# First batch's column sums in two tiles, early small work on two engines, and other steps for three pieces of side work in a fused attention and FFN kernel

## The chip, the cores and the metric

The kernel runs on one core of one Trainium2 chip. The metric is the device time of one execution in microseconds (us); "before" is the median of three runs.

## What is computed

Four batches of q, k and v, each 6080 x 256, go through an attention over channels, and its result through a two-layer FFN with squared ReLU:

```python
qn = q / (np.linalg.norm(q, axis=1, keepdims=True) + 1e-06)
kn = k / (np.linalg.norm(k, axis=1, keepdims=True) + 1e-06)
s = kn.transpose(0, 2, 1) @ qn / tau
s = s - s.max(-1, keepdims=True)
a = np.exp(s)
a /= a.sum(-1, keepdims=True) + 1e-09
x = (v @ a).reshape(B * S, D)
h = np.maximum(x @ w_in, 0.0)
out = h * h @ w_out            # w_in 256 x 2048, w_out 2048 x 256, both float64
```

The norms run over the 6080 rows, so each needs the sum of squares of a whole column of q or k.

## The kernel before

Since `x @ w_in = v @ (a @ w_in)`, each batch first forms the 256 x 256 product of k and q (the "gram"), the softmax from it, and W = a @ w_in; then the 6080 rows of v pass in 12 blocks of up to 512 rows through W, ReLU, square and w_out. Every product is taken from high and low parts (fp32r), except the gram of the first batch and of the first five chunks of the second (the "heads"), which are plain float32.

**Start (`start_first`).** q and k of batch 0 come in 25 chunks of 512 KB (the last two smaller), one k and one q transfer each, all issued by SP; SP's issues wait for the landing of the transfer eight places before. Ten chunk buffers are used in turn, so chunk c + 9 is asked for at step c. Per chunk TensorE makes four 128x256 products into `gram` (each shown as two matmuls in the trace), ScalarE squares the chunk (`squares`, chunk 0 straight into the tile `acc`, the others into a tile "x" with two buffers), and VectorE adds the square to `acc` (`add_squares`, one step later). In between, w_in's first 1 MB piece is loaded and decoded from float64 (`Weights.load`, `Weights.stage`, `decode`), a few instructions at a time. The products of the last three chunks are kept back (`rest`).

**Softmax and W (`softmax_and_W(0)`, lines 403 to 540).** VectorE adds the two halves of `acc`; TensorE sums it over the partitions (`ps_n`); a chain of small VectorE operations makes the norms, then come scaling, exponential, transposes (`ps_t`) and W's first quarter (`ps_w`). While TensorE would wait it is given the kept-back products and the ten rows of the heads (`head_products`; a row is two products, so four matmuls of the trace); the list `beside_first` says at which step of the chain, and the loop at lines 771 and 772 issues the two rows that are left before the blocks begin.

**Blocks.** The order is one list of steps, each a block's 128 columns of the hidden layer (`first_product`: six 128x512 matmuls into `ps_h`). Two steps are a pair. ScalarE takes ReLU from PSUM (x), squares a pair, and copies its high part (`g_hi`); VectorE subtracts for the low part (`g_lo`); two pairs later TensorE multiplies by w_out into `ps_o`. The first two blocks (32 steps, `PAIR`) use w_out directly, eight products per pair. From the third block on seven products per pair are used (`by_seven`): VectorE makes four sums of x's quarters, and TensorE needs seven combinations of w_out, four of which (`wS_hi`, `wS_lo`) are made once by `sums_of_w_out`: four groups of three steps (an addition; four short operations; ScalarE's copy to `wS_hi` with VectorE's subtraction to `wS_lo`). During the first two blocks the remaining pieces of w_in and w_out are decoded (`stages`), W's quarters are formed at steps 6, 14 and 22, the heads are squared and added (`head_squares`, one chunk per call) and `sums_of_w_out` follows: lines 812 and 813 call one or the other once per step after step 24. What is left goes on from step 32 (`beside`), one call per step except at two steps of each block, and then the attention of batch 1 (`attention(1)`) from its sixth chunk.

Each engine works its instructions in program order, so an instruction that waits holds all behind it on that engine.

Of the kernel before, what the change touches and what calls it, by code (L numbers as in the profile page):

```python
# [8 lines left out]
F32 = mybir.dt.float32  # L9
# [4 lines left out]
AF = mybir.ActivationFunctionType  # L14
# [16 lines left out]
def kernel(  # L31
# [22 lines left out]
    tensor, vector, scalar, pool_engine = (  # L54
        InProgramOrder(tc, e) for e in (nc.tensor, nc.vector, nc.scalar, nc.gpsimd)
    )
    P = 128
    B, N, C = q.shape
# [3 lines left out]
    T = 512  # L62
# [3 lines left out]
    J = 2  # L66
# [28 lines left out]
    const = ctx.enter_context(tc.tile_pool(name="const", bufs=1))  # L95
    wpool = ctx.enter_context(tc.tile_pool(name="wpool", bufs=NG))
    pool = ctx.enter_context(tc.tile_pool(name="pool", bufs=2))
    ps_acc = ctx.enter_context(tc.tile_pool(name="ps_acc", bufs=2, space=bass.MemoryType.PSUM))
    ps_h = ctx.enter_context(tc.tile_pool(name="ps_h", bufs=3, space=bass.MemoryType.PSUM))
# [4 lines left out]
    ones = const.tile([P, P], F32, name="ones")  # L104
# [3 lines left out]

    exp_bias = const.tile([P, 1], F32, name="exp_bias")
    vector.memset(exp_bias, -896.0 * 2.0**23)  # L110
    wo_hi = const.tile([P, NF, C], F32R, name="wo_hi")
    wo_lo = const.tile([P, NF, C], F32R, name="wo_lo")
    late = {}
# [126 lines left out]
    class Gram:  # L240
# [45 lines left out]
        def squares(self, c):  # L286
            p, jn, _ = self.q[c]
            if c == 0:
                self.acc = pool.tile([P, 2, J, C], F32, tag="acc", name=f"acc{self.b}", bufs=1)
                sq = self.acc  # L290
            else:

                sq = self.raws[c]
                if self.b == 0:
                    sq = pool.tile([P, 2, J, C], F32, tag="x", name=f"sq{self.b}_{c}")
                self.sq[c] = sq
            scalar.activation(sq[:p, :, :jn, :], self.raws[c][:p, :, :jn, :], AF.Square)

        def add_squares(self, c):
            p, jn, _ = self.q[c]  # L300
            if c in self.sq:
                a = self.acc[:p, :, :jn, :]
                vector.tensor_add(a, a, self.sq.pop(c)[:p, :, :jn, :])

    grams = {}
# [1 line left out]
    def start_first(b=0):  # L307

        g = grams[0] = Gram(0)
        total = g.n + HEAD  # L310
        AHEAD = len(FAST_TAGS) - 1

        room = pool.tile([P, HEAD - 1, 2, J, C], F32, tag="wS_lo", name="qk_heads", bufs=1)

        def load(c):
            if c == g.n:
                grams[1] = Gram(1)
            if c < g.n:
                g.load(c, FAST_TAGS[c % len(FAST_TAGS)])
            elif c < total and B > 1:  # L320
                grams[1].load(c - g.n, raw=room[:, c - g.n] if c - g.n < HEAD - 1 else None)

        for c in range(AHEAD):
            load(c)
        for c in range(g.n):
            if c < g.n - LAST:
                for _ in g.products(c, [(g.raws[c], g.raws[c])]):
                    pass
            g.squares(c)
            if c:  # L330
                g.add_squares(c - 1)
            load(c + AHEAD)
            if c in (2, 15):
                weights.load(int(c > 2))
            if c in (13, 14, 15, 17):
                weights.stage(0)
            if c == 19:
                load_v(*order[0])
        for c in range(g.n + AHEAD, total):
            load(c)  # L340
        g.add_squares(g.n - 1)

        def rest():
            for c in range(g.n - LAST, g.n):
                for _ in g.products(c, [(g.raws[c], g.raws[c])]):
                    pass
            yield

        return rest()

    def head_products():

        g = grams[1]
        for c in range(HEAD):
            yield from g.products(c, [(g.raws[c], g.raws[c])])

    def head_squares():
        g = grams[1]
        while g.raws:
            c = min(g.raws)  # L360
            g.squares(c)
            del g.raws[c]
            g.add_squares(c)
            yield
# [182 lines left out]
    def load_v(b, n, tag="v"):  # L547
        t0, tn = blocks[n]
        raw = pool.tile([P, NC, T], F32, tag=tag, name=f"v{b}_{n}", bufs=1)
        nc.sync.dma_start(raw[:, :, :tn], vT[b, :, t0 : t0 + tn].rearrange("(c p) t -> p c t", p=P))  # L550
        V[b, n] = [raw, None, None]
# [10 lines left out]
    def split_v_lo(b, n):  # L562
        tn = blocks[n][1]
        raw, hi, _ = V[b, n]
        V[b, n][2] = pool.tile([P, NC, T], F32R, tag="v_lo", name=f"v_lo{b}_{n}")
        vector.tensor_sub(V[b, n][2][:, :, :tn], raw[:, :, :tn], hi[:, :, :tn].bitcast(F32))
# [8 lines left out]
    def first_product(b, n, f):  # L575
        tn = blocks[n][1]
        _, v_hi, v_lo = V[b, n]
        w_hi, w_lo = W[b, f // FPG]
        f0 = (f % FPG) * P
        ps = ps_h.tile([P, T], F32, tag="h", name=f"ps_h{b}_{n}_{f}")  # L580
        parts = [(c, x, y) for x, y in ((w_hi, v_hi), (w_hi, v_lo), (w_lo, v_hi)) for c in range(NC)]
        for i, (c, wt, vt) in enumerate(parts):
            tensor.matmul(
                ps[:, :tn], wt[:, c, f0 : f0 + P], vt[:, c, :tn], start=i == 0, stop=i == len(parts) - 1
            )
        if f % 2 == 0:
            X[b, n, f // 2] = pool.tile([P, 8, tn // 2], F32, tag="x", name=f"x{b}_{n}_{f // 2}")
        x = X[b, n, f // 2].rearrange("p s t -> p (s t)")
        s = slice((f % 2) * tn, (f % 2 + 1) * tn)
        scalar.activation(x[:, s], ps[:, :tn], AF.Relu)  # L590
# [21 lines left out]
    def parts_of_sums(b, n, r):  # L612

        x = X.pop((b, n, r))
        hi, lo = G[b, n, r]
        if by_seven(b, n):
            hi, lo, src = hi[:, 3:7, :], lo[:, 3:7, :], x[:, 4:8, :]
        else:
            src = x[:, 0:4, :]
        scalar.copy(hi, src)  # L620
        vector.tensor_sub(lo, src, hi.bitcast(F32))
# [3 lines left out]
    def second_product(b, n, r, part):  # L625
        if by_seven(b, n):
            seven_products(b, n, r, part)
        else:
            eight_products(b, n, r, part)
# [115 lines left out]

    weights = Weights()
    rest = start_first()
    first = softmax_and_W(0)
    heads, squares_of_heads = (head_products(), head_squares()) if B > 1 else (iter(()), iter(()))
# [16 lines left out]
    while (0, 0) not in W:  # L766
# [1 line left out]
        for piece in beside_first.get(at, ()):  # L768
            piece()
        at += 1  # L770
    for _ in heads:
        pass


    stages = {0: [1, 2], 1: [2, 1], 2: [2, 2], 3: [2], 4: [2, 2], 5: [2]}
# [19 lines left out]
    for i in range(len(steps) + 2 * LAG):  # L795
        part = now["part"] = i % 2
        if i < len(steps):
            b, n, f = steps[i]
            at = b * NB + n
            first_product(b, n, f)  # L800
            if n == NB - 1 and f % FPG == FPG - 1:
                may_write_W.add((b + 1, f // FPG))

        if i >= PAIR:
            gens = (beside,)
        else:
            for item in stages.get(i, ()):
                weights.stage(item)
            if i == 1:
                split_v_lo(*order[1])  # L810
            gens = (first,) if i in steps_of_W else ()
            if i > 24:
                gens += (squares_of_heads if B > 1 and grams[1].raws else sums,)

        if i >= PAIR and steps[min(i, len(steps) - 1)][2] in (2 * LAG - 2, 2 * LAG - 1):
            gens = ()
        if i < PAIR or part == 0:
            for gen in gens:
                next(gen, None)
        if part == 0 and 0 <= i // 2 - 1 < len(pairs):  # L820
            parts_of_sums(*pairs[i // 2 - 1])
        if i in steps_of_W:
            next(first)
        if part == 1 and i // 2 < len(pairs):
            squares_and_sums(*pairs[i // 2])
        if part and late_work:
            if next(late_work[0], "end") == "end":
                late_work.pop(0)
        if i >= 2 * LAG:
            second_product(*pairs[i // 2 - LAG], part)  # L830
        if i < len(steps):
            at_hi, at_lo = (None, None) if at == 0 else (12, 13) if at == 1 else (6, 8)
            if i == 2 and len(order) > 2:
                load_v(*order[2])
            if f == at_hi and at + 1 < len(order):
                split_v_hi(*order[at + 1])
            if f == at_lo and at + 1 < len(order):
                split_v_lo(*order[at + 1])
                if at + 2 < len(order):
                    load_v(*order[at + 2])  # L840
        if i >= PAIR and part:
            for gen in gens:
                next(gen, None)
# [27 lines left out]
```

## Time and profile before

| | |
|---|---|
| median of 3 runs | 2225.31 us (2223.28 to 2227.23) |
| profiled execution, its own time | 2223.41 us |
| its span, first to last instruction | 2221.6 us |
| TensorE (PE) busy | 2207.7 us (99%) |
| ScalarE (ACT) busy | 1844.9 us (83%) |
| VectorE (DVE) busy | 1762.6 us (79%) |
| granted TensorE clock over the span | 1.000 |

The 1.8 us between span and time lie around the program. Nearly all instructions stand under line 27, the helper that issues them, so one goes by tile names and times. A matmul's shown duration overlaps the next one's; from one start to the next is what it costs.

### The profile page before, as it was taken

How to read it: one execution, taken by the hardware profiler on the slowest of the kernel's cores; microseconds unless marked ns; L12 is line 12 of the kernel's file. 1: busy time of each engine (PE TensorE's matmuls, PEld its weight loads, DVE VectorE, ACT ScalarE, POOL GpSimd, SP SyncE). 2: the span in 40 equal slices, each digit the busy share in tenths (PEclk: the TensorE clock that was granted, in tenths of full speed). 3: DMA queues.
4: the chain of work that ended last, by engine and by line, in shares of the span. 5: the costliest groups of instructions: out<-in, count | busy, mean ns of one | idle time of the engine just before them, and what ended most of it. 6: DMA issues, size and time to landing. Idle time of an engine off the chain costs nothing.

```text
span 2221.6 us, 34359 instructions
## 1 busy us (share of the span) xinstructions
PE 2207.7 (99%) x13740; PEld 1982.9 (89%) x13740; DVE 1762.6 (79%) x2470; ACT 1844.9 (83%) x2294; POOL 0.7 (0%) x6
## 2 busy tenths in 40 slices
PE   9999999999999999999999999999999999999999
PEld 7788999988989999988898999998899888888888
DVE  7868888888778888878777888887877787787783
ACT  5788888888788888888878888888887888888885
POOL 0000000000000000000000000000000000000000
PEclk9999999999999999999999999999999999999999
DMA  9510122110111112110121122110102010010000
GB/s 342 176 67 29 60 74 68 46 39 29 66 66 58 60 61 71 62 41 22 35 70 54 60 68 73 58 53 22 33 24 76 21 36 20 22 37 20 22 26 18
DMA packets 76495, 126.99 MB, mean 57 GB/s; under 512 B 7728, under 2 KB 34096, under 8 KB 76336
## 3 DMA queue, kind: packets, MB, share of 16 engines
q1 hardware_dynamic: 76336, 124.81, 17.2%
q8 instruction: 107, 1.75, 0.3%
q14 instruction: 52, 0.43, 0.1%
HBM read 95.68 MB, written 29.10 MB: 56 GB/s over the span
## 4 chain that ended last, share of the span: by engine, by line
PE 95%; DVE 3%; DMA 1%; ACT 1%; issue 0%; SPq 0%; DVEq 0%; ACTq 0%
PE ps_h L27 46%; PE ps_o L27 41%; PE gram L27 5%; PE ps_w L27 2%; DVE g_lo L27 1%; DMA qk<-in_k 1%; DVE acc L27 1%; DVE x L27 0%; ACT x L27 0%; DMA qk<-in_q 0%; ACT g_hi L27 0%; PE ps_n L27 0%; DVE o L27 0%; DVE dec_m L27 0%; DVE wo_sums L27 0%
## 5 line engine op out<-in xcount | busy, mean ns | idle before, releaser
L27 DVE TENSOR_TENSOR g_lo<-x,g_hi 128x768 fp32r<-128x768 f32 (+2 forms) x744 | 804.7, 1082 | 94.2 <-ACT g_hi L27 93.9
L27 DVE TENSOR_TENSOR x<-x 128x256 f32<-128x256 f32 (+3 forms) x1080 | 551.9, 511 | 276.9 <-ACT x L27 251.9
L27 ACT CAST g_hi<-x 128x768 fp32r<-128x768 f32 (+2 forms) x744 | 698.0, 938 | 23.4 <-DVE x L27 10.9
L27 ACT ACTIVATE x<-ps_h 128x512 f32<-128x512 f32 (+1 forms) x768 | 456.3, 594 | 298.9 <-PE ps_h L27 277.2
L27 PE MATMUL ps_h<-v_hi,w_hi 128*128 128x512 f32 (+1 forms) x1536 | 479.3, 393 | 0.0
L27 PE MATMUL ps_h<-v_hi,w_lo 128*128 128x512 f32 (+1 forms) x1536 | 477.5, 391 | 0.0
L27 PE MATMUL ps_h<-v_lo,w_hi 128*128 128x512 f32 (+1 forms) x1536 | 474.9, 390 | 0.0
L27 ACT ACTIVATE x<-x 128x1024 f32<-128x1024 f32 (+1 forms) x384 | 404.6, 1054 | 12.2
L27 PE MATMUL ps_o<-g_lo,wS_hi 128*128 128x256 f32 (+1 forms) x1440 | 402.7, 280 | 3.1 <-DVE g_lo L27 2.8
L27 PE MATMUL ps_o<-g_hi,wS_lo 128*128 128x256 f32 (+1 forms) x1440 | 401.6, 279 | 0.0
L27 PE MATMUL ps_o<-g_hi,wS_hi 128*128 128x256 f32 (+1 forms) x1440 | 401.1, 279 | 0.0
L27 PEld LDWEIGHTS ps_h<-v_lo,w_hi 128*128 128x128 f32 x1536 | 287.9, 187 | 65.4
L27 PEld LDWEIGHTS ps_h<-v_hi,w_lo 128*128 128x128 f32 x1536 | 288.5, 188 | 62.1
L27 PE MATMUL ps_o<-g_hi,wo_hi 128*128 128x256 f32 (+3 forms) x1176 | 330.6, 288 | 0.9 <-ACT g_hi L27 0.9
L27 PE MATMUL ps_o<-g_hi,wo_lo 128*128 128x256 f32 (+3 forms) x1176 | 330.7, 288 | 0.0
L27 PE MATMUL ps_o<-g_lo,wo_hi 128*128 128x256 f32 (+3 forms) x1176 | 330.4, 287 | 0.1
L27 PEld LDWEIGHTS ps_o<-g_lo,wS_hi 128*128 128x128 f32 x1440 | 271.1, 188 | 19.7 <-DVE g_lo L27 3.9
L27 PEld LDWEIGHTS ps_o<-g_hi,wS_hi 128*128 128x128 f32 x1440 | 270.4, 188 | 15.5
L27 PEld LDWEIGHTS ps_o<-g_hi,wS_lo 128*128 128x128 f32 x1440 | 270.6, 188 | 0.0
L27 PEld LDWEIGHTS ps_h<-v_hi,w_hi 128*128 128x128 f32 x1536 | 239.3, 188 | 4.9
L27 PEld LDWEIGHTS ps_o<-g_hi,wo_hi 128*128 128x128 f32 x1176 | 221.4, 188 | 17.4 <-ACT g_hi L27 1.4
L27 PEld LDWEIGHTS ps_o<-g_lo,wo_hi 128*128 128x128 f32 x1176 | 220.8, 188 | 16.7 <-DVE g_lo L27 0.5
(87 smaller groups left out, 1669.0 us busy)
## 6 DMA issues: line engine op xcount, KB each, us to landing
v<-in_vT SPq DMA_DIRECT2D x44, 512.0 KB, 3.8
qk<-in_k SPq DMA_DIRECT2D x87, 256.0 KB, 2.7
qk<-in_q SPq DMA_DIRECT2D x87, 256.0 KB, 3.0
out_T<-o SPq DMA_DIRECT2D x168, 128.0 KB, 1.7
wi_hi<-wi_kept SPq DMA_DIRECT2D x12, 512.0 KB, 3.3
wi_lo<-wi_kept SPq DMA_DIRECT2D x12, 512.0 KB, 4.1
w_raw<-in_w_in SPq DMA_DIRECT2D x4, 1024.0 KB, 5.2
w_raw<-in_w_out SPq DMA_DIRECT2D x4, 1024.0 KB, 5.4
```

The source lines that it names most:

```text
L27: return lambda *args, **kwargs: self.tc.keep_in_program_order(issue(*args, **kwargs))
```

## The change

```diff
@@ setup
     exp_bias = const.tile([P, 1], F32, name="exp_bias")
     vector.memset(exp_bias, -896.0 * 2.0**23)
+
+    for _ in range(7):
+        tensor.matmul(ps_h.tile([P, T], F32, tag="h", name="ps_first")[:, 0:P], ones, ones, start=True, stop=True)
+    scalar.activation(const.tile([P, 1], F32, name="first"), exp_bias, AF.Square)
@@ Gram.squares
             if c == 0:
                 self.acc = pool.tile([P, 2, J, C], F32, tag="acc", name=f"acc{self.b}", bufs=1)
+                self.accs = [self.acc]
                 sq = self.acc
+            elif c == 1 and self.b == 0:
+                sq = pool.tile([P, 2, J, C], F32, tag="g_hi", name=f"acc{self.b}_1")
+                self.accs.append(sq)
@@ Gram.add_squares
-                a = self.acc[:p, :, :jn, :]
+                a = self.accs[c % len(self.accs)][:p, :, :jn, :]
@@ start_first
-            if c in (2, 15):
-                weights.load(int(c > 2))
-            if c in (13, 14, 15, 17):
+            if c in (0, 15):
+                weights.load(int(c > 0))
+            if c in (12, 13, 14, 16):
                 weights.stage(0)
@@
         g.add_squares(g.n - 1)
+        vector.tensor_add(*g.accs[:1], *g.accs)
@@ main program
-    for _ in heads:
-        pass
@@ loop over steps
+            if i in (2, 3):
+                next(heads, None)
             gens = (first,) if i in steps_of_W else ()
-            if i > 24:
+            if i >= 16 and (i >= 24 or i % 2 == 0):
                 gens += (squares_of_heads if B > 1 and grams[1].raws else sums,)
```

In words: seven products of a tile of ones (fourteen matmuls in the trace) and one small square are issued ahead of the first q and k. In batch 0, squares of even chunks are added into one tile and those of odd chunks into another, and the two tiles are added at the end. w_in's first piece is asked for after chunk 9 rather than after chunk 11, and four of its decoding steps come one chunk earlier. The last two rows of the heads move into steps 2 and 3. The squares of the heads begin at step 16 (one in each even step, then one in each step from 24), so that the sums of w_out begin at step 25 rather than 30 and the attention of batch 1 five calls earlier.

Three places show how the instructions move. VectorE, the end of batch 0's sums, before (`acc` is the tile of sums, `sq_n` a chunk's squares):

```order
L27 TENSOR_TENSOR acc_132<-acc_132,sq_21_348 128x1024
L27 TENSOR_TENSOR acc_132<-acc_132,sq_22_351 128x1024
L27 TENSOR_TENSOR acc_132<-acc_132,sq_23_354 128x2x256
L27 TENSOR_TENSOR acc_132<-acc_132,sq_24_357 64x2x256
L27 TENSOR_TENSOR acc_132<-acc_132 128x2x256
```

and of the change (`acc_1_158` is the second tile):

```order
L27 TENSOR_TENSOR acc_148<-acc_148,sq_22_366 128x1024
L27 TENSOR_TENSOR acc_1_158<-acc_1_158,sq_23_369 128x2x256
L27 TENSOR_TENSOR acc_148<-acc_148,sq_24_372 64x2x256
L27 TENSOR_TENSOR acc_148<-acc_148,acc_1_158 128x1024
L27 TENSOR_TENSOR acc_148<-acc_148 128x2x256
```

Neighbouring additions go into different tiles now, and one full-size addition stands before the halves are added.

TensorE, from the heads to the fifth step of the blocks (`gram_301` and `gram_316` are batch 1's gram, `qk_4` the heads' last chunk), before:

```order
L27 MATMUL gram_301<-qk_heads 128x256 x4
L27 MATMUL gram_301<-qk_4_341 128x256 x4
L27 MATMUL ps_h_0_0_490<-v_hi_0_414,w_hi_0_458 128x512 x2
...
L27 MATMUL ps_h_0_2_519<-v_hi_0_414,w_lo_0_459 128x512 x2
L27 MATMUL ps_h_0_3_534<-v_hi_0_414,w_hi_0_458 128x512 x2
...
L27 MATMUL ps_h_1_0_547<-v_hi_1_447,w_hi_0_458 128x512 x2
```

and of the change:

```order
L27 MATMUL gram_316<-qk_heads 128x256 x4
L27 MATMUL ps_h_0_0_502<-v_hi_0_430,w_hi_0_474 128x512 x2
...
L27 MATMUL ps_h_0_2_531<-v_hi_0_430,w_lo_0_475 128x512 x2
L27 MATMUL gram_316<-qk_4_356 128x256 x2
L27 MATMUL ps_h_0_3_548<-v_hi_0_430,w_hi_0_474 128x512 x2
...
L27 MATMUL gram_316<-qk_4_356 128x256 x2
L27 MATMUL ps_h_1_0_563<-v_hi_1_463,w_hi_0_474 128x512 x2
```

The four products of `qk_4` stood ahead of the first `ps_h`; two now follow the third step and two the fourth.

VectorE, the last group of w_out's sums with no other work between the four short operations and the subtraction, before (fourth pair of the third block, `x_2_3`):

```order
L27 TENSOR_TENSOR x_2_3_1337<-x_2_3_1337 128x512
L27 TENSOR_TENSOR x_2_3_1337<-x_2_3_1337 128x256 x2
L27 TENSOR_TENSOR g_lo_2_3_1364<-x_2_3_1337,g_hi_2_3_1363 128x768
L27 SCALAR_TENSOR_TENSOR wo_sums_1340<-wo_1339 128x256
L27 TENSOR_TENSOR wo_sums_1340<-wo_1339 128x256
L27 SCALAR_TENSOR_TENSOR wo_sums_1340<-wo_sums_1340,wo_1339 128x256
L27 TENSOR_TENSOR wo_sums_1340<-wo_1339,wo_sums_1340 128x256
L27 TENSOR_TENSOR wS_lo<-wo_sums_1340,wS_hi 128x4x256
L27 TENSOR_TENSOR g_lo_2_3_1364<-x_2_3_1337,g_hi_2_3_1363 128x1024
```

and of the change (third pair, `x_2_2`, and what follows it):

```order
L27 SCALAR_TENSOR_TENSOR wo_sums_1315<-wo_1314 128x256
L27 TENSOR_TENSOR wo_sums_1315<-wo_1314 128x256
L27 SCALAR_TENSOR_TENSOR wo_sums_1315<-wo_sums_1315,wo_1314 128x256
L27 TENSOR_TENSOR wo_sums_1315<-wo_1314,wo_sums_1315 128x256
L27 TENSOR_TENSOR wS_lo<-wo_sums_1315,wS_hi 128x4x256
L27 TENSOR_TENSOR g_lo_2_2_1338<-x_2_2_1312,g_hi_2_2_1337 128x1024
L27 TENSOR_TENSOR x_2_3_1369<-x_2_3_1369 128x512
L27 TENSOR_TENSOR x_2_3_1369<-x_2_3_1369 128x256 x2
L27 TENSOR_TENSOR g_lo_2_3_1395<-x_2_3_1369,g_hi_2_3_1394 128x768
L27 TENSOR_TENSOR qk_lo_5_1430<-qk_5_1414,qk_hi_5_1429 128x1024
L27 TENSOR_TENSOR g_lo_2_3_1395<-x_2_3_1369,g_hi_2_3_1394 128x1024
```

Before, a fourth group followed this one in the next pair; now this is the fourth group, one pair earlier, and batch 1's first low part (`qk_lo`) follows it.

## Rows read from the trace of the kernel before

**Rows 1.** The page, part 1: busy us, share of the span, instructions.

```profile
PE 2207.7 (99%) x13740; PEld 1982.9 (89%) x13740; DVE 1762.6 (79%) x2470; ACT 1844.9 (83%) x2294; POOL 0.7 (0%) x6
```

**Rows 2.** TensorE's waits, whole run: for whom, us in total, times, longest.

```profile
PE gram L27 <- DMA qk<-in_q: 4.3, 1, 4.3
PE ps_o L27 <- DVE g_lo L27: 2.8, 2, 1.9
PE ps_o L27 <- ACT g_hi L27: 0.9, 1, 0.9
PE ps_n L27 <- DVE acc L27: 0.8, 1, 0.8
PE ps_w L27 <- DVE wi_lo L27: 0.5, 1, 0.5
```

**Rows 3.** Timeline, TensorE, 4.2 to 44.7: start, us, operation, count, idle before.

```profile
4.32 4.50 PE L27 MATMUL gram<-qk 128*128 128x256 f32 x9 [4.32 <-DMA qk<-in_q]
...
8.61 36.37 PE L27 MATMUL gram<-qk 128*128 128x256 f32 x167
```

**Rows 4.** Windows: us, busy of PE, PEld, DVE, ACT, POOL, clock, DMA, GB/s.

```profile
0.00:45.80 45.80, 40.66 (x176) 34.67 (x176) 31.39 (x31) 28.30 (x28) 0.70 (x6) 1.00 0.95 340
...
107.50:132.40 24.90, 24.90 (x109) 20.27 (x108) 17.55 (x18) 19.37 (x24) 0.00 (x0) 1.00 0.17 60
```

**Rows 5.** Timeline, SP's issues and ScalarE's squares, 38 to 44.

```profile
40.74 0.33 SPq L264 DMA_DIRECT2D qk_heads<-in_k  x1
...
40.84 1.06 ACT L27 ACTIVATE sq<-qk 128x1024 f32<-128x1024 f32 x1 [0.27 <-DVE acc L27]
```

**Rows 6.** Chain that ended last, up to 75: start, us, what.

```profile
42.23 1.24 DVE acc L27
...
43.56 0.70 DVE acc L27
...
45.82 1.05 PE ps_n L27 x8
```

**Rows 7.** Timeline, VectorE, 34.5 to 35.7.

```profile
34.46 1.22 DVE L27 SCALAR_TENSOR_TENSOR dec_e<-w_raw,dec_e 128x1024 int32<-128x1024 int32 x1
35.60 1.22 DVE L27 TENSOR_TENSOR acc<-acc,sq 128x1024 f32<-128x1024 f32 x1
```

**Rows 8.** Timeline, all engines, 60 to 80.

```profile
61.88 1.89 PE L27 MATMUL gram<-qk 128*128 128x256 f32 x8
...
63.36 1.23 DVE L27 TENSOR_TENSOR dec_m<-dec_m,dec_e 128x1024 f32<-128x1024 f32 x1
...
65.69 1.04 ACT L27 CAST wo_hi<-dec_m 128x1024 fp32r<-128x1024 f32 x1
...
70.53 1.05 ACT L27 CAST g_hi<-x 128x1024 fp32r<-128x1024 f32 x1
...
71.63 0.73 PE L27 MATMUL ps_o<-g_hi,wo_hi 128*128 128x512 f32 x2 [0.95 <-ACT g_hi L27]
...
79.71 0.73 PE L27 MATMUL ps_w<-wi_lo,eT_hi 128*128 128x512 f32 x2 [0.55 <-DVE wi_lo L27]
```

**Rows 9.** Timeline, 115 to 120, VectorE and TensorE.

```profile
115.01 1.23 DVE L27 TENSOR_TENSOR g_lo<-x,g_hi 128x1024 fp32r<-128x1024 f32 x1 [2.00 <-ACT g_hi L27]
...
118.09 0.63 PE L27 MATMUL ps_o<-g_lo,wo_hi 128*128 128x512 f32 x2
```

**Rows 10.** Timeline, 179 to 195, third block.

```profile
179.84 1.61 DVE L27 TENSOR_TENSOR x<-x 128x512 f32<-128x512 f32 x3
...
183.81 1.05 ACT L27 CAST wS_hi<-wo_sums 128x1024 fp32r<-128x1024 f32 x1 [2.65 <-DVE wo_sums L27]
...
184.89 1.23 DVE L27 TENSOR_TENSOR wS_lo<-wo_sums,wS_hi 128x1024 fp32r<-128x1024 f32 x1 [1.12 <-ACT wS_hi L27]
...
187.31 0.39 PE L27 MATMUL ps_o<-g_lo,wS_hi 128*128 128x256 f32 x1 [0.96 <-DVE g_lo L27]
...
194.69 0.39 PE L27 MATMUL ps_o<-g_lo,wS_hi 128*128 128x256 f32 x1 [1.87 <-DVE g_lo L27]
```

## The prediction

> **What bounds the kernel now.** The page's first part comes first: TensorE is busy 99% of the span [rows 1]. So the question is only where it waits, or runs slowly, and whether the change touches those places. The view of TensorE's waits over the whole run answers it: 4.3 us until the first q lands, then five waits of 5.0 us together, 0.8 + 0.9 + 0.5 + 2.8 [rows 2]. Besides there is a slow start: nine matmuls begin within 4.29 us (4.32 to 8.61), then 167 follow in 36.37, 0.218 each [rows 3]. The profile grants the clock as 1.00 there too, but twice the pace is what the 1.2 and 2.4 GHz levels differ by. Everything else is TensorE working at its pace, and no part of the change removes a matmul. So the change can win about 5.0 us plus at most 4.29 - 9 x 0.218 = 2.3 us.
>
> The timeline then shows what each wait hangs on: the last additions into the sums of squares before ps_n at 45.82 [rows 6], the first pair's g_hi at 71.63 and W's second quarter at 79.71 [rows 8], and two low parts in the third block, at 187.31 and 194.69 [rows 10].
>
> Differences are taken against the profiled execution (2223.41 us, span 2221.6), which is 1.9 us under the median of 2225.31; I apply the sum to the median. About 0.2%, 4.5 us, is what a measurement of this kernel can tell from no change.
>
> **Small products of ones; table load early.** The ones are ready when the first q is not, so the fourteen small matmuls cost nothing unless they last past 4.32; at half the slow matmuls' pace (half the columns, 0.24 each) they take 3.3 us from about 1.0. TensorE can then start at its full pace. What it gains is limited by arrival, and arrival does not change: the transfer engines are 95% occupied at 340 GB/s up to 45.8 [rows 4]. But TensorE is not what ps_n waits for: its last product before ps_n was done 0.8 us ahead [rows 2]. A faster TensorE only waits longer. The same holds for ScalarE's table load. I book **0**; the ends are 0 and the -2.3 above, the latter only if ps_n came earlier as well.
>
> **Two tiles of sums.** Into one tile, additions start 1.33 us apart (42.23 to 43.56 for one of 1.24) [rows 6]; an addition after an instruction that it does not depend on starts 1.14 after it (34.46, 35.60) [rows 7]. So 0.19 us per full addition is to be had, as long as VectorE is what is late. At the end it hardly is. SP's issue at 40.74 is the one that waits for chunk 22's q (eight places before), and ScalarE's square of that chunk starts at 40.84 already [rows 5]. In the new order: square 22 at 40.82 to 41.88, its addition to 43.12; chunk 24's square needs the buffer of square 22, as before, so 43.15 to 43.78; chunk 23's addition lies in that time, chunk 24's ends at 44.50. Then the new addition of the two tiles, 0.10 + 1.23, to 45.83, and the halves, 0.04 + 0.70, to 46.57. ps_n starts at 46.61 instead of 45.82: **0.8 us later**. The other end: with arrival no limit, the six full additions from 35.60 on each gain 0.19, together 1.1, against 1.33 for the addition that is new: +0.2. Arrival is in the rows, so I take +0.8. Asking for w_in two chunks earlier moves 1 MB ahead of chunks 10 and 11 and leaves all later arrivals where they are; its decoding one chunk earlier is hidden the same way.
>
> From ps_n to 61.88 TensorE has work throughout (kept-back products, heads), so all of this is later by the same 0.8.
>
> **Heads' rows in steps 2 and 3.** Eight matmuls at 0.216, 1.73 us (61.88 to the first ps_h at 63.42, the last one overlapping) [rows 8], leave the path to the first ps_h, which starts at 62.7 instead of 63.4. What counts is when the first g_hi is ready. ScalarE is busy without a gap from 65.19 to its end at 71.58, and the second piece in that stretch is the copy wo_hi at 65.69, whose input VectorE has at 63.36 + 1.23 = 64.59. Now ScalarE is there earlier, but the input comes at 65.38. So g_hi comes 65.69 - 65.41 = **0.3 us earlier**, not 1.7. TensorE, with 1.73 us of products moved in, reaches the place at 71.5 and hardly waits. From g_hi to W's low part at 79.66 VectorE and ScalarE follow each other through nine instructions; so the wait at 79.71 ends 0.3 us earlier too. Behind it TensorE has no wait until 187. Up to here the sum is **-0.3** (ends: -1.1 if ps_n is not late, +0.3 if the wait at 71.63 stays and its successor too).
>
> **Heads' squares at steps 16 to 24.** Five squares of 1.06 us on ScalarE [rows 5] and four additions of 1.23 on VectorE come into a stretch in which they have 5.5 and 7.3 us free of 24.9 [rows 4]. Queued behind them are g_hi and g_lo. At step 18 g_lo ends at 116.24 and TensorE takes it at 118.09: 1.85 us of slack [rows 9]; the square ahead of it takes 1.06. I book **0**; the ends are 0 and what the slower rival costs. At steps 24 to 29, where that work was, it makes room.
>
> **w_out's sums earlier.** Both late waits come from them. In the fourth pair VectorE has, between x's sums at 179.84 and the second g_lo, four short operations, 1.12 us of idling for ScalarE's wS_hi, and wS_lo; and ScalarE stands 2.65 us ahead of wS_hi, which makes the next pair's x late [rows 10]. That costs 0.96. In the fifth pair another addition and four short operations cost 1.87. In the new order one such bunch is left, in the third pair, with the same neighbours: I expect **about 1.0 us of waiting there still**. In the pair behind it there is one low part (1.22 us) instead of 1.22 + 1.46, and six products of batch 1's gram give VectorE 0.7 us more per pair: no second wait. So **-1.9** (ends: 0 and -2.8).
>
> **Sum:** -0.3 - 1.9 = **-2.2 us**, 2223.1 us.
>
> **A rule that speaks against it.** After the faster start TensorE stands idle from about 44.1 to 46.6, three times the 0.84 us before ps_n now, after which the rows show full pace at once. The Trainium skill, "TensorE: Matmul & The Clock Gate", Part 1, says that an idle array falls back to 1.2 GHz and must earn the full clock again. No run here shows a wait of that length. It is a rival below.
>
> **The rivals.**
> (1) **All waits go:** the sums come into place ahead of ps_n, g_hi is early, the third block keeps up: -5.0 [rows 2], 2220.3, and part of the slow start on top, 2219. For it: each edit aims at a row of that view. Against: arrival, and the bunch that is still there.
> (2) **The late waits only move:** the bunch in the third pair and v's parts behind it cost what two bunches did: the 1.9 is lost, 2225.0.
> (3) **The clock falls in the longer wait:** nine matmuls at the pace of the start cost 2.3 us more [rows 3], all of it on the path: 2225.4.
> (4) **Slower:** squares and additions of the heads hold g_hi and g_lo, 1.06 + 1.23 = 2.29 per step. It decides where both delays add up past the 1.85 of slack [rows 9]: 0.44 at the first of the four steps with an addition, 2.29 at each later one if nothing is caught up, 7.3 in all, less 2.2: 2230.4. Against: the free time above.
>
> That the change does not do what it says is contained in (2) and in the sums' two tiles, which by my working give nothing.
>
> **How the numbers follow.** Forecast 0.52, (1) 0.16, (2) 0.16, (3) 0.08, (4) 0.08. Faster by over 0.2% is (1) and a little of the forecast's spread, 0.18; slower is (4), 0.08; within it 0.74. The range takes the forecast with its ends (-0.3 to -2.8 with up to 0.8 more either way), (2), (3), part of (1) and the spread of the runs: 2219.8 to 2226.5.
>
> **What would show it.** Right: ps_n starts at about 46.6 and waits for acc by 2 us or more; the pitch is 0.216 from the second chunk on; no wait over 0.3 at 71; a wait of some 0.7 near 79.4; one wait of about 1.0 on g_lo near 182 and none near 190. Wrong: ps_n before 45.8; a pitch of 0.43 after it; any wait of TensorE between 107 and 132; two waits or none in the third block.

## The result, and the profile after

The change takes **2227.72 us** (median of 20 runs, 2225.60 to 2230.19) against **2224.56 us** (20 runs, 2223.28 to 2227.23; the 2225.31 of the prediction is the median of its first three): ratio 1.0016, 95% interval 1.0009 to 1.0023. So it is slower by 3.2 us, outside the range, and on the other side than forecast. The profiled execution took 2227.85 us, span 2226.1. One execution of the change has a mean granted clock of 1.000 and took 2225.60; the nineteen others, at 0.998 or 0.999, took 2226.8 to 2230.2.

The waits of TensorE in the profile of the change, over the whole run (for whom, us in total, times, longest), as [rows 2]:

```profile
PE ps_n L27 <- DVE acc L27: 2.5, 1, 2.5
PE gram L27 <- DMA qk<-in_q: 1.1, 2, 0.7
PE ps_o L27 <- DVE g_lo L27: 1.1, 2, 0.7
PE ps_first L27 <- DVE exp_bias L27: 1.1, 1, 1.1
PE ps_w L27 <- DVE wi_lo L27: 0.6, 1, 0.6
```

By this view alone the change has won: g_hi's wait of 0.9 is gone, the two for g_lo fell from 2.8 to 1.1, and only ps_n waits longer. The loss lies where TensorE is busy. The timeline of TensorE shows the first part of it, and the windows view (us, busy of PE, PEld, DVE, ACT, POOL, granted clock, DMA share, GB/s) the reason:

```profile
47.09 1.02 PE L27 MATMUL ps_n<-ones,acc 128*128 128x1 f32 x8 [2.48 <-DVE acc L27]
47.97 5.58 PE L27 MATMUL gram<-qk 128*128 128x256 f32 x16
```

```profile
44.00:47.00 3.00, 0.61 (x3) 0.19 (x1) 2.84 (x5) 0.24 (x1) 0.00 (x0) 1.00 1.05 389
...
48.00:52.00 4.00, 4.00 (x12) 3.26 (x13) 3.38 (x20) 0.00 (x0) 0.00 (x0) 0.58 1.05 386
```

TensorE idles 2.48 us, and then the granted clock is 0.58 on average over 48 to 52: mostly the 1.2 GHz level, in place of 2.4. The sixteen matmuls of the trace behind ps_n (the kept-back products) take 5.58 us, where the kernel before takes 3.90 for them:

```profile
46.74 3.90 PE L27 MATMUL gram<-qk 128*128 128x256 f32 x16
```

The second part is in no wait and in no clock. Take one stretch that both kernels work through alike, from one copy on ScalarE to one sum on VectorE 1585 us later. In the timelines these two stand, for the kernel before,

```profile
575.48 0.79 ACT L27 COPY o<-ps_o 128x768 f32<-128x768 f32 x1
...
2160.33 1.15 DVE L27 TENSOR_TENSOR o<-o 128x256 f32<-128x256 f32 x2
```

and for the change

```profile
577.24 0.79 ACT L27 COPY o<-ps_o 128x768 f32<-128x768 f32 x1
...
2164.94 1.14 DVE L27 TENSOR_TENSOR o<-o 128x256 f32<-128x256 f32 x2
```

1584.85 us before, 1587.70 after: **2.85 us more** for the same instructions, with TensorE busy but for some tenths and the clock at 1.00. It accrues evenly over the stretch. I call it the length of the long stretch below. (The expectations name lengths some 0.4 us shorter, 1584.4 and 1587.3; only differences are used.)

### The profile page after: what moved, and what is told of

It reads as the page before. It is cut to its first block, busy times and chain, and to the rows that moved or that the text cites. A ratio compares the mean times of both kernels' runs of the same rounds, so it can differ in the third digit from the quotient of the medians.

```text
span 2226.1 us, 34367 instructions
## 1 busy us (share of the span) xinstructions
PE 2215.4 (100%) x13754; PEld 1988.2 (89%) x13754; DVE 1762.5 (79%) x2470; ACT 1845.0 (83%) x2295; POOL 0.7 (0%) x6
## 3 DMA queue, kind: packets, MB, share of 16 engines
q8 instruction: 108, 1.77, 0.3%
## 4 chain that ended last, share of the span: by engine, by line
PE 94%; DVE 3%; ACT 1%; DMA 1%; issue 0%; SPq 0%; DVEq 0%; ACTq 0%
PE ps_h L27 46%; PE ps_o L27 41%; PE gram L27 5%; PE ps_w L27 2%; DVE g_lo L27 1%; DVE acc L27 1%; DVE x L27 1%; DMA qk<-in_k 1%; ACT x L27 0%; DMA qk<-in_q 0%; ACT g_hi L27 0%; DVE dec_m L27 0%; DVE o L27 0%; PE ps_n L27 0%; ACT sq L27 0%
```

## The experiments

Every time is a median, unless one execution is named. Each set was timed on one chip beside the kernel before, which had 2225.04 (33 runs) in the first set, 2224.06 (33) in the second and 2223.70 (26) in the fourth. The ratios compare with it. The change was timed apart from these sets, so "less than the change", and any other difference between sets, is good to about 1 us.

**First set: what of the two parts at the start, and is it the place of the tiles?** The change allocates a four-byte tile ahead of all large ones, which moves them by 32 bytes.

shift_only: the kernel before, with `const.tile([P, 1], F32, name="first")` behind the memset of `exp_bias`, unused.

> The kernel before with one unused tile of four bytes per partition, laid out ahead of wo_hi, so that all later tiles lie 32 bytes further; no instruction is added. The trace of the change has every matmul a little slower for the rest of the run: it falls behind the kernel before by 2.9 us from 600 to 2190 us without a wait. Theory P (placement of the tiles does it): 1.5 to 3 us above the kernel before, as a steady drift from 600 on. Theory C (the clock after the wait ahead of ps_n, and run-to-run spread, explain the result): no difference beyond 0.05%, 1 us.

2224.73 (11 runs), ratio 1.0000 (0.9991 to 1.0009); the long stretch is as before. The 32 bytes cost nothing.

first_64:

```diff
-    scalar.activation(const.tile([P, 1], F32, name="first"), exp_bias, AF.Square)
+    scalar.activation(const.tile([P, 16], F32, name="first")[:, 0:1], exp_bias, AF.Square)
```

> The change with its one four-byte tile made 64 bytes wide, so that the later tiles lie where they did modulo 64 bytes; no instruction is altered. Theory P: 1.5 to 3 us less than the change, 2224.5 to 2226.5, and no drift against the kernel before from 600 on. Theory C: as the change, about 2228.

2226.97 (11 runs), ratio 1.0011 (1.0002 to 1.0020): hardly less than the change, and the long stretch is as long as there. That the later tiles lie where they did modulo 64 bytes changes nothing, so this alignment is not it. In this profile q came earlier, ps_n waited 0.9 us only, and the clock held.

no_warm: the loop of seven `ps_first` matmuls taken out.

> The change without its seven small matmuls of ones. Theory C (the long idle time before ps_n drops the clock): the slow matmuls are back at the start, TensorE is done with the chunks later and idles under 2 us, the ten matmuls behind ps_n run at 0.216 in place of 0.43, ps_n stays at 47.1: 2.0 us less than the change, about 2226. Rival (the idle time would have dropped the clock anyway, arrival being the limit): as the change, 2228.

2225.55 (11 runs), 2.2 less than the change; ratio to before 1.0005 (0.9996 to 1.0014). TensorE in its timeline:

```profile
46.14 1.05 PE L27 MATMUL ps_n<-ones,acc 128*128 128x1 f32 x8 [1.17 <-DVE acc L27]
47.05 3.90 PE L27 MATMUL gram<-qk 128*128 128x256 f32 x16
```

The clock holds, as theory C said, but ps_n did not stay at 47.1: it comes 0.95 earlier. That I had not expected. (In the fourteen profiles without the small matmuls ps_n comes at 45.55 to 46.55, so a few tenths between two profiles say nothing; 47.09 lies outside.) The delay shows in ScalarE's timeline. Here is the change, with its squares of the chunks behind w_in:

```profile
23.18 1.06 ACT L27 ACTIVATE sq<-qk 128x1024 f32<-128x1024 f32 x1 [2.87 <-DMA qk<-in_q]
25.35 1.06 ACT L27 ACTIVATE sq<-qk 128x1024 f32<-128x1024 f32 x1 [1.11 <-DMA qk<-in_q]
```

and no_warm:

```profile
22.97 1.06 ACT L27 ACTIVATE sq<-qk 128x1024 f32<-128x1024 f32 x1 [2.87 <-DMA qk<-in_q]
24.32 1.06 ACT L27 ACTIVATE sq<-qk 128x1024 f32<-128x1024 f32 x1 [0.30 <-DMA qk<-in_q]
```

In the change, one q lands 0.8 us late between 23 and 25, and everything behind it keeps that delay. The DMA view has the one 16 KB fetch of instructions of the first 45 us (count, MB, share; the whole run has 108 such packets, 1.77 MB) in the window 21 to 23 of the change,

```profile
q8 instruction: 1, 0.02, 3.3%
```

and in 36 to 38 before, 34 to 36 in no_warm. All six kernels with the small matmuls have it from 22 to 24, the fourteen without them from 34 to 38. So fourteen more matmuls bring the fetch forward, from the end of q's stream into its middle. That the fetch holds up the q behind it is a likely reading, not shown. The step from the first of these two squares to the next is 2.2 to 2.6 us in four of the six, and 1.34 to 1.36 in all fourteen others; but in first_64 and kept_layout the fetch comes early too and the step is 1.3, and in kept_layout ps_n is late all the same. In the profiles of one_tile, kept_layout and second_tile_in_g_lo ps_n comes at 46.98 to 47.26; in first_64 at 46.10.

one_tile: the branch that makes `acc0_1` and the joining addition taken out.

> The change with one tile of sums, as before, and without the addition that joins the two. Theory C with the sum's own step (the joining addition makes ps_n 0.8 to 1.3 us late): ps_n at 45.8 to 46.1, TensorE idles 1.2 to 1.5 us ahead of it; if the clock still holds after that, 3 us less than the change, 2225; if it falls, 1.2 us less, 2226.8. Rival (arrival is a little later in the change for another reason, as w_in's earlier load): ps_n stays at 46.5 or later, 2227.5.

2223.96 (11 runs), 3.8 less than the change; ratio 0.9999 (0.9991 to 1.0008). It came near the lower of theory C's times (2225), and against both of its readings: ps_n is not early (47.18, wait 2.13), and the clock falls (0.68 in 48 to 52). 2.9 of the 3.8 us come from the long stretch, which is as before (1584.81). So the two tiles bring its lengthening, and the joining addition is not what makes ps_n late: without it one q is late as well, by a step of 2.19.

**Second set: the layout.** A tag's buffers are laid out where the tag is first used. The change takes its second tile of sums from g_hi's tag, at the second chunk; so g_hi's two buffers (14 KB per partition) now lie ahead of x's, and x, v_hi and v_lo lie 14 KB further; g_lo stays.

layout_only:

```diff
                 self.acc = pool.tile([P, 2, J, C], F32, tag="acc", name=f"acc{self.b}", bufs=1)
                 sq = self.acc
+                if self.b == 0:
+                    pool.tile([P, 2, J, C], F32, tag="g_hi", name=f"acc{self.b}_1")
```

> The kernel before with one unused tile taken from g_hi's tag where the change takes its second tile of sums: no instruction is added, but g_hi's two buffers now lie ahead of x, v_hi and the others, as in the change, and these 14 KB further per partition. The three kernels with two tiles fall behind the kernel before by 2.8 us between 600 and 2190 us, evenly and without a wait; those with one tile don't. Theory L (the place of the buffers does it): the same 2.8 us of drift here, 2.8 us above the kernel before (0.13%). Rival (the drift is the second tile's work, or a state that a run falls into): no drift, as before within 1 us.

2230.97 (11 runs), ratio 1.0024 (1.0015 to 1.0033): with no instruction added the kernel before is 6.9 us slower. Its long stretch is 1587.74, 2.9 longer, as theory L said:

```profile
580.58 0.80 ACT L27 COPY o<-ps_o 128x768 f32<-128x768 f32 x1
...
2168.32 1.14 DVE L27 TENSOR_TENSOR o<-o 128x256 f32<-128x256 f32 x2
```

The other 4 us are more than the theory gave and lie ahead of the stretch: in its profile the clock also fell twice, behind ps_n (wait 1.1) and behind the second wait for g_lo (1.9), and the blocks ahead of the stretch run at the slower pace too (1.2 us, by kept_layout below).

kept_layout: the change, and ahead of `acc0_1` an unused tile of every tag in the old order.

> The change, all instructions kept, with unused tiles taken in the old order ahead of the second tile of sums, so that g_hi, x, v_hi and the others lie where the kernel before has them (plus 32 bytes). Theory L: no drift from 600 on; 2.8 us less than the change, about 2225, and still with the clock's fall behind ps_n. Rival: as the change, 2227.7.

2223.84 (11 runs), 3.9 less than the change; ratio 0.9998 (0.9989 to 1.0006). Its two ends of the long stretch give 1584.76:

```profile
575.85 0.79 ACT L27 COPY o<-ps_o 128x768 f32<-128x768 f32 x1
...
2160.61 1.15 DVE L27 TENSOR_TENSOR o<-o 128x256 f32<-128x256 f32 x2
```

All of the change's instructions are in it, and in its profile ps_n comes as late (46.98) and the clock falls as well, so its 3.9 us are the place: 2.9 in the long stretch and 1.2 ahead of it, where from the heads' first product (53.33, in the change 53.48) to the copy it takes 522.52 us and the change 523.76. Beside one_tile (2223.96) the two tiles as work cost nothing that can be told from these medians.

keep_warm:

```diff
+        if b == 0:
+            for _ in range(16):
+                tensor.matmul(ps_h.tile([P, T], F32, tag="h", name="ps_warm")[:, 0:P], ones, ones, start=True, stop=True)
         ps_n = ps_h.tile([P, T], F32, tag="h", name=f"ps_n{b}")
```

> The change with sixteen small matmuls of ones (1.8 us at full pace) in TensorE's queue ahead of ps_n, in the time in which it waits for acc. Theory C (the idle time drops the clock): the matmuls behind ps_n run at 0.216, the granted clock stays 1.00 from 48 to 52, 2 us less than the change where its clock falls, about 2226. Rival (something else, as the transfers at that time, slows them): still 0.43 behind ps_n, 2227.7 or above.

2226.98 (11 runs, 2226.21 to 2228.16), 0.7 less than the change. TensorE's timeline, and the window of 48 to 52:

```profile
44.37 3.73 PE L27 MATMUL ps_warm<-ones 128*128 128x128 f32 x32
47.94 0.95 PE L27 MATMUL ps_n<-ones,acc 128*128 128x1 f32 x8
48.76 3.89 PE L27 MATMUL gram<-qk 128*128 128x256 f32 x16
```

```profile
48.00:52.00 4.00, 4.00 (x23) 3.38 (x23) 2.62 (x17) 0.00 (x0) 0.00 (x0) 1.00 1.05 386
```

Theory C is shown: at the same time and with the DMA as busy (1.05, 386 GB/s in both) the matmuls run at full pace (clock 1.00 in 48 to 52). The price was mine: each of the sixteen counts twice in the trace, 3.73 us in place of 1.8, so ps_n came 0.85 late. The spread is also under half of the change's.

one_tile_no_warm: both edits at the start undone.

> The change with one tile of sums and without the seven matmuls of ones: what is left are w_in's earlier load and the other steps of the heads' rows, their squares and w_out's sums. Theories L and C: no drift, no fall of the clock behind ps_n, the waits at 71.6 and 194.7 gone: 2 to 2.5 us under the kernel before, 2222 to 2223. Rival (the two edits at the start have no part in it): as the kernel before or above, 2225.

**2221.34** (11 runs, ten of them from 2220.59 to 2221.50), ratio 0.9985 (0.9976 to 0.9993): faster than the kernel before by 2.7 us. Its waits:

```profile
PE gram L27 <- DMA qk<-in_q: 4.4, 1, 4.4
PE ps_o L27 <- DVE g_lo L27: 1.1, 2, 0.7
PE ps_n L27 <- DVE acc L27: 0.8, 1, 0.8
PE ps_w L27 <- DVE wi_lo L27: 0.5, 1, 0.5
```

**Third set: four layouts** of the kernel before, by unused tiles as in layout_only; one execution each, so read by the long stretch, not by the time.

lay_g_hi_before_v_lo: g_hi's buffers just ahead of v_lo's.

> The kernel before, no instruction altered, with g_hi's buffers laid out just ahead of v_lo's: v_lo lies 14 KB further, as in the change, g_hi 8 KB nearer, x and v_hi stay. What is read is the drift against the kernel before from 600 to 2190 us. Theory VL (v_lo's place costs it): 2.8 us. Theory VH (v_hi's place or x's): none. Theory G (g_hi, far ahead, costs it): none.

1584.80, no difference, although v_lo lies where it does in the change: theory VL falls.

lay_v_lo_first: v_lo's buffers ahead of x's.

> The kernel before, no instruction altered, with v_lo's buffers laid out ahead of x's: x and v_hi lie 8 KB further, v_lo 62 KB nearer, g_hi and g_lo stay. Drift from 600 to 2190 us: theory VL: none, or a gain of some us, as v_lo is then at the nearest place; theory VH: 1 to 3 us; theory G: none.

1581.94: 2.9 shorter, which theory VL alone had allowed; VH's 1 to 3 more fell.

lay_g_lo_first: g_lo's buffers ahead of x's.

> The kernel before, no instruction altered, with g_lo's buffers laid out ahead of x's in place of g_hi's: x, v_hi and v_lo lie as in the change, g_lo is where g_hi is there and g_hi where g_lo was. Drift from 600 to 2190 us: theories VL and VH: 2.8 us, as in the change; theory G: none.

1581.51: 3.3 **shorter**, with x, v_hi and v_lo just where the change has them. Against VL and VH, and none of my theories had a gain. g_hi first costs 2.9, g_lo first gains 3.3.

lay_v_hi_last: v_hi's buffers behind all others.

> The kernel before, no instruction altered, with v_hi's buffers laid out last: v_hi lies 48 KB further, all between 8 KB nearer, x stays. Drift from 600 to 2190 us: theory VH by v_hi's place: 3 us or more; theory VL: none or a gain; theory G: none.

1589.26: 4.4 longer, as VH said; but VH had failed in the two layouts before.

**Fourth set: the place used, and two single parts.**

second_tile_in_g_lo, one word of the change:

```diff
-                sq = pool.tile([P, 2, J, C], F32, tag="g_hi", name=f"acc{self.b}_1")
+                sq = pool.tile([P, 2, J, C], F32, tag="g_lo", name=f"acc{self.b}_1")
```

> The change, whole, with one word altered: its second tile of sums is taken from g_lo's tag in place of g_hi's, so that g_lo's buffers lie where the change has g_hi's. Theory L: a gain of 3 us from 600 to 2190 us in place of a loss of 2.8: about 2222, under the kernel before, with everything that the change does at the start still in it. Rival: as the change, 2227.7.

**2219.63** (10 runs), ratio 0.9976 (0.9967 to 0.9985): 8.1 us less than the change, though its profile has the wait of 2.48 ahead of ps_n and the fallen clock (0.58) like the change's. The long stretch, 1581.57:

```profile
575.44 0.79 ACT L27 COPY o<-ps_o 128x768 f32<-128x768 f32 x1
...
2157.01 1.14 DVE L27 TENSOR_TENSOR o<-o 128x256 f32<-128x256 f32 x2
```

The groups of TensorE's matmuls from 600 to 2190 (x, busy us, mean ns) differ by up to 6 ns, some shorter here, some longer, so no one group carries the difference. The change:

```profile
L27 PE MATMUL ps_h<-v_hi,w_hi 128*128 128x512 f32 (+1 forms) x1141 | 359.2, 396 | 0.0
...
L27 PE MATMUL ps_o<-g_lo,wS_hi 128*128 128x256 f32 (+1 forms) x1140 | 320.1, 281 | 0.2
...
L27 PE MATMUL ps_o<-g_hi,wS_lo 128*128 128x256 f32 (+1 forms) x1140 | 316.7, 278 | 0.0
```

and this kernel:

```profile
L27 PE MATMUL ps_h<-v_hi,w_hi 128*128 128x512 f32 (+1 forms) x1146 | 354.6, 390 | 0.0
...
L27 PE MATMUL ps_o<-g_hi,wS_lo 128*128 128x256 f32 (+1 forms) x1139 | 319.8, 281 | 0.0
...
L27 PE MATMUL ps_o<-g_lo,wS_hi 128*128 128x256 f32 (+1 forms) x1139 | 315.5, 277 | 0.2
```

best_g_lo_first: one_tile_no_warm with one unused tile of g_lo's tag behind `acc0`.

> The change with one tile of sums and without the matmuls of ones (2221.3 by itself), and g_lo's buffers laid out ahead of x's by one unused tile. Theory L (the place of g_hi and g_lo sets the pace of the long part): from 600 to 2190 us it gains a further 3 us on the kernel before, about 2218.3, 6 us under the kernel before. Rival (the single runs of the layouts were lucky, or the gain belongs to the old order of instructions): 2221.3.

**2216.82** (5 runs, 2216.41 to 2216.96), ratio 0.9964 (0.9951 to 0.9978): 6.9 us under the kernel before, the best of all. It is 1.5 under what was expected: the long stretch, 1581.58, gains 3.2 on one_tile_no_warm as theory L said, and in the profiles the work ahead of and behind it gains another 1.0.

w_in_back: one_tile_no_warm with w_in's load and stages at their old chunks.

> As the kernel with one tile of sums and without the matmuls of ones (2221.3), with w_in's load and its four decoding stages put back to chunks 2, 13, 14, 15 and 17. My prediction booked the edit at 0: 2221.3, ps_n at the same time within 0.2 us. Rival (w_in ahead of chunks 10 and 11 makes the additions late): ps_n 0.2 to 0.4 us earlier, 2221.0. Rival on the other side (it makes room later): ps_n over 0.5 us later.

2221.21 (11 runs) against 2221.34, and ps_n 0.2 later in the one profile, within the spread: the edit is worth nothing that can be told, as booked.

heads_back: one_tile_no_warm with the heads' last two rows ahead of the first step.

> As the kernel with one tile of sums and without the matmuls of ones (2221.3), with the heads' last two rows back ahead of the first step. By the trace of that kernel the wait on the first pair's g_hi (0.9 to 1.1 us in the kernel before) is gone, not 0.3 us shorter as I had predicted. If the moved rows do that: the wait of about 1 us at 71 returns and the run is 0.8 to 1.1 us longer, 2222.2. Rival (the heads' squares and sums, or the start, do it): no wait there, 2221.3.

2222.23 (11 runs), 0.9 more, and the wait is back:

```profile
71.50 0.73 PE L27 MATMUL ps_o<-g_hi,wo_hi 128*128 128x512 f32 x2 [0.95 <-ACT g_hi L27]
```

So the moved rows do take it away.

**Last: what of the place does it?** Two more layouts of the kernel before, one execution each.

lay_swap_g: g_hi's and g_lo's buffers exchanged.

> The kernel before, no instruction altered, with the places of g_hi's and g_lo's buffers exchanged (14 KB per partition each); all else stays. The same stretch of work, from the copy at 575.5 to the sum at 2160.3, takes 1584.4 us in the old order, 1587.3 with g_hi first, 1581.2 with g_lo first. Theory S (g_lo lying below g_hi is what gains): 1581 to 1582 here. Rival (their distance from x, v_hi or the weights matters): 1584 or above.

1584.86, no difference: g_lo below g_hi is not what gains; theory S falls.

lay_g_both_first: g_hi's, then g_lo's buffers ahead of x's.

> The kernel before, no instruction altered, with g_hi's and then g_lo's buffers ahead of x's: both below x, v_hi and v_lo, g_hi below g_lo as in the old order. The same stretch: theory S: 1584 to 1585, since their order is the old one. Rival (g_hi below x and v is what costs): 1587 or above; rival (g_lo below x and v is what gains): 1582 or less.

1598.93, 14.1 longer, in one run of 2243.92. The rival that g_hi below x and v costs allowed a loss, but gives no reason for one so large. So none of the theories tried here, of one buffer's place or of the order of g_hi and g_lo, explains the lengths from 1581.5 to 1598.9. What the pace depends on **stays open**; that it is the place alone is shown by layout_only, kept_layout and second_tile_in_g_lo.

## Why the prediction was wrong

- **Small products of ones, booked at 0: the step that failed first.** "A faster TensorE only waits longer" is right as far as it goes; ps_n waited 2.48, as I said. But I took the longer wait for free in the forecast. The matmuls of ones cost 2.2 us (the change against no_warm) to 2.6 (one_tile against one_tile_no_warm), each good to about 1: 1.7 of it is the sixteen matmuls at the lower clock (5.58 against 3.90), 0.95 the later ps_n. The first part is rival (3), to which I gave 0.08; that its price of 2.3 is near the whole is luck, since it holds nothing for the later ps_n. A slower pace behind ps_n was also among my signs of being wrong. By the rule of the Trainium skill, "TensorE: Matmul & The Clock Gate", Part 1, that an idle array falls back to 1.2 GHz, the traces agree: the granted clock fell after the waits of 2.0 us and more ahead of ps_n (four profiles of four). My ground for holding it unlikely, full pace at once after 0.84 us, spoke of a wait a third as long.
- **"Arrival does not change": wrong.** An instruction fetch came into q's stream. With fourteen more matmuls on TensorE, one q was 0.8 us late in the middle of the stream, and ps_n 0.95; that the fetch is the reason is not shown.
- **The place of the second tile: a term that was not in the sum.** I counted its additions and not its address. It costs 3.9 us (the change against kept_layout), more than everything else: without it the change is level with the kernel before (kept_layout), not 2.2 us under it.
- **Two tiles as work, +0.8: too large.** It is +0.1, near the +0.2 that I had only as the other end. VectorE's last nine additions, the joining one and the halves in the change,

```profile
35.30 9.65 DVE L27 TENSOR_TENSOR acc<-acc,sq 128x1024 f32<-128x1024 f32 x9
44.99 1.23 DVE L27 TENSOR_TENSOR acc<-acc,acc 128x1024 f32<-128x1024 f32 x1
46.25 0.69 DVE L27 TENSOR_TENSOR acc<-acc 128x512 f32<-128x512 f32 x1
```

and with one tile in one_tile_no_warm:

```profile
34.47 10.80 DVE L27 TENSOR_TENSOR acc<-acc,sq 128x1024 f32<-128x1024 f32 x9
45.30 0.69 DVE L27 TENSOR_TENSOR acc<-acc 128x512 f32<-128x512 f32 x1
```

From the first addition to the halves it takes 10.95 us against 10.83: the faster pace of the additions pays for nearly all of the one that joins the tiles. I had arrival as the limit here; in the change the nine follow each other without a gap. Its ps_n is late because the first of them starts 0.8 us later than here.

- **Heads' rows: right but for ps_n.** -1.1 with ps_n on time, of which 0.8 was to be lost by it; heads_back has -0.9. In the change the wait at 71 is gone although ps_n is late. In one_tile_no_warm g_hi's copy starts at 69.69, 0.84 ahead of the kernel before [rows 8].
- **w_out's sums: right in size, in part by luck.** One wait of about 1.0 was to stay near 182 and none near 190; there is one of 0.38, and a new one of 0.70 that I did not foresee, in the attention of batch 1, where ScalarE has waited for its nr:

```profile
183.89 0.38 PE L27 MATMUL ps_o<-g_lo,wS_hi 128*128 128x256 f32 x1 [0.38 <-DVE g_lo L27]
...
481.64 0.39 PE L27 MATMUL ps_o<-g_lo,wS_hi 128*128 128x256 f32 x1 [0.70 <-DVE g_lo L27]
```

2.8 became 1.1: -1.7 for -1.9. On top comes what I did not see: behind the wait of 1.9 at 194 the clock falls in some executions of the old instructions. The windows of 195 to 199 in two of them, the kernel before and shift_only:

```profile
195.00:199.00 4.00, 4.00 (x26) 3.53 (x25) 3.93 (x6) 3.08 (x5) 0.00 (x0) 1.00 0.00 0
```

```profile
195.00:199.00 4.00, 4.00 (x18) 3.54 (x17) 3.93 (x6) 2.90 (x4) 0.00 (x0) 0.57 0.00 0
```

- **Heads' squares, w_in: 0, right.** TensorE waits nowhere between 107 and 132; w_in_back shows no gain. Rival (4) is dead.

The moves that I had priced at -1.1 (with ps_n on time) and -1.9 bring -2.7 (one_tile_no_warm); the matmuls of ones +2.4 and the place of the tile +3.9 make it about +3.6, against +3.2 measured. These terms come from different sets, so the agreement is no closer than about 1 us.

## What to carry to other kernels

A buffer's first use can move all others: after an edit that allocates, time the layout apart from the work, with unused tiles, and try two or three layouts; here that spans more than all the edits. Work that makes an engine reach a wait sooner isn't free: look at what the idle time does to its clock, and at whether an instruction fetch has moved among the transfers. An experiment with one part undone would have read as "the two tiles are slow"; only the same instructions at the old places told it apart.

## What the hardware showed that was not expected

- The pace of TensorE, busy and at a granted clock of 1.00, depends on where its operands and the tiles written beside it lie: 1581.5 to 1598.9 us for the same stretch; among the kernels of one layout it agrees within 0.1 us (1584.76 to 1584.86 in eight with the old order, the last two places exchanged or not; 1587.70 to 1587.77 in five with g_hi first; 1581.51 to 1581.58 in three with g_lo first). The Trainium skill, "SBUF — State Buffer", "Who interferes with whom", says that TensorE and ScalarE never wait for another engine's access. No run here tells whether TensorE waits for an access or for something else that the place decides; that a layout is free for TensorE, as one would read from it, the measurement refutes.
- Of two executions with a wait of 1.9 us at the same place, one kept the clock (before) and one lost it (shift_only); 1.1 us ahead of ps_n lost it once (layout_only), 1.2 and 1.4 to 1.5 did not (no_warm; shift_only, lay_g_lo_first and lay_g_both_first). The length of the wait alone does not decide.
- Fourteen more matmuls and their weight loads moved a 16 KB fetch from 34 to 38 us (fourteen profiles) to 22 to 24 (six). The Trainium skill, "Runtime: NRT & Kernel Launch", "Instruction fetch mechanics", has such blocks of 16 KiB and calls their cost mostly hidden; here a step of 2.2 to 2.6 us in place of 1.35 in the stream of q stands beside the fetch in four profiles of the six, the change among them, and none in first_64 and kept_layout.
